# Scaling w_in on VectorE, and transposing the attention output by DMA from the third block of 512 tokens on

## The chip, the cores and the metric

One core of a Trainium2 chip. The metric is the device time of one launch in microseconds (us). All runs told of here were correct against the reference and fell in the fast state (a run over 1.5% above the fastest of the same kernel would be called slow). The profile covers one execution; its span is about 1.7 us shorter than the time of that launch. The two profiled launches compared first, 353.62 us before and 342.93 after, are each some 1.1 us faster than the median of their kernel. Shorthand in profile lines: PE is TensorE's matmuls, PEld its weight loads, DVE VectorE, ACT ScalarE, POOL GpSimd, SP the engine that issues the transfers (SPq its queue); L117 is line 117 of that kernel's source.

## The reference

```python
scores = q @ k.T / sqrt(64)                  # 8 batches, 8 heads, 576 positions, 64 per head
attn   = softmax(scores masked to 0 <= row - column < 64)
x      = (attn @ v), heads side by side      # 4608 tokens x 512
out    = (relu(x @ w_in) ** 2) @ w_out       # w_in 512 x 2048, w_out 2048 x 512
```

## The kernel before

The 4608 tokens are handled in 36 attention blocks of 128 tokens, `i`, four of which make one of the nine feed-forward blocks of 512 tokens, `g`. Four things matter.

The weights: `w_in` comes as sixteen tiles of 128x512 through four staging buffers, and each is scaled and cast.

```python
ws = wst.tile([P, FQ], FP32, name="ws", tag="ws")          # wst: bufs=4
nc.sync.dma_start(out=ws[:], in_=moe_w_in[c * P:(c + 1) * P, quar * FQ:(quar + 1) * FQ])
nc.gpsimd.tensor_scalar(out=w_in_sb[:, c, quar * FQ:(quar + 1) * FQ], in0=ws[:],
                        scalar1=W_SCALE, scalar2=None, op0=ALU.mult)
```

The attention of one block of 128 tokens: `transposes` (q and k), `scores` (with ScalarE's exponential and VectorE's mask, `pm`), `values` (giving `x_sb`), and last the transposition of `x_sb`, which the up-projection needs as `xT`:

```python
def to_xT(i):
    xt = ps_att.tile([P, DMC, P], FP16, name="xt_ps", tag="ps_a")
    for c in range(DMC):                                   # DMC = 4
        nc.tensor.transpose(out=xt[:, c, :], in_=xs[i][:, 2 * c:2 * c + 2, :], identity=ident[:])
    nc.vector.tensor_copy(out=xT_of(i // 4)[:, :, (i % 4) * P:(i % 4 + 1) * P], in_=xt[:])
```

The feed-forward: `ffn_up(g)` makes 16 groups of four matmuls (`hps`), each followed by a relu on ScalarE (`hrelu`) and a product on VectorE (`h`), over two accumulators. `ffn_out(g)` makes four output tiles of sixteen matmuls (`ops`), also over two accumulators, each emptied by ScalarE (`osb`).

The order: the first eight attention blocks (`NFIRST`) run in a start phase, with a quarter-wide up-projection per block (`ffn_up_chunk`). Then comes one stage per feed-forward block, in which streams are woven together:

```python
load(0)
for s in load_w_in():
    s()
for i in range(1, NV - 1):
    load(i)
...
for s in load_w_out() + ffn_up_chunk(0):
    s()
T(1), S_(1), warm(2), V(1), T(2), warm(2), X(1), S_(2)     # attention of block 1
...
for g in range(1, NTB + 1):
    streams = [(ffn_out(g - 1), 0.0, 1.0)]
    if g >= 2 and g < NTB:
        streams.append((ffn_up(g), 0.0, 1.0))
    if g + 1 < NTB:
        streams.append((attention(g + 1), 0.0, 0.95))
    if g + 2 < NTB:
        streams.append((loads(g + 2), 0.0, 1.0))
    for s in weave(*streams):
        s()
```

This is the order in which the program is written. The builder then orders each engine's instructions by itself, so a change of one operation can move others; "built order" below means what came out of that.

The softmax here doesn't subtract the row's maximum and nothing guards it: scores larger than these inputs give would overflow.

## Time and profile before

| | before |
|---|---|
| time, median of 3 runs | 354.94 us (354.49 to 355.84) |
| span of the profiled run | 351.9 us |
| last of the sixteen w_in scalings starts | 32.0 us, on GpSimd |
| TensorE busy in the whole span | 329.0 us, idle 22.9 us |

What bounds it is told in the prediction, with its lines. For the comparison a cut into three stretches is more useful than fixed times. The cuts are the starts of ScalarE's eviction of the fourth output tile (end of the first stage) and of the twelfth (end of the third stage). Columns of this table of windows: from:to, length, then busy us with the instruction count for PE, PEld, DVE, ACT and POOL, then granted clock, DMA share, GB/s.

```profile
0.00:98.41 98.41, 79.46 (x1062) 57.26 (x1064) 51.11 (x144) 39.59 (x69) 79.03 (x115) 0.90 0.85 218
98.41:169.69 71.28, 71.16 (x678) 36.56 (x678) 49.55 (x123) 36.95 (x67) 29.45 (x47) 1.00 0.54 129
169.69:351.90 182.21, 178.36 (x1412) 87.18 (x1410) 99.87 (x225) 87.62 (x154) 36.35 (x60) 1.00 0.33 88
```

Length minus TensorE's busy time is its idle time: 18.95 us in the first stretch, 0.12 in the second, 3.85 in the third. The second stretch is as full as a stretch can be, and so it is the one to watch when work is taken out of it. How the output matmuls of stage 2 (operand `h_1087`) lie in it is seen in the group of those instructions, with duration min/median/max in ns and the first and last start:

```profile
L296 PE MATMUL ops<-w_out_sb,h_1087 x64: 379/379/390, 98.8 to 135.2; 128*128 128x512 f16 x64
```

They are spread over 36 us, between the up-projection's matmuls of the same stage. While one group of four up-projection matmuls waits for relu and product, TensorE has output matmuls to do.

### The profile page before, as it was taken

Reading aid. Unit: us, or ns where it says so; the run is one execution under the profiler, and the core shown is the slowest. Engines: PE = TensorE matmul, PEld = TensorE weight load, DVE = VectorE, ACT = ScalarE, POOL = GpSimd, SP = SyncE. Lnnn points to the kernel's source line nnn. Section 1 sums busy time; section 2 is a strip of 40 time slices with the busy share of each in tenths; the row PEclk is TensorE's granted clock in tenths of the full one; section 3 lists DMA queues with packets and bytes.
Section 4 is the critical chain, followed back from the end, with each engine's and each line's share of the span. In section 5 each row is a group of like instructions: output and inputs, shape, how many; then the busy total and the mean of one; then the engine's idle time right before and its main releaser. Section 6 shows DMA issues by size and latency. Waiting matters only on the chain.

```text
span 351.9 us, 7908 instructions
## 1 busy us (share of the span) xinstructions
PE 329.0 (93%) x3146; PEld 181.0 (51%) x3146; DVE 200.5 (57%) x490; ACT 164.2 (47%) x289; POOL 144.8 (41%) x220
## 2 busy tenths in 40 slices
PE   4837898999999999999999999999999999999995
PEld 1424687885554555544554454445445544444442
DVE  3222588883385586767576756665676566633300
ACT  2112357553536554654555355536653664344411
POOL 4999997569575123324476464550000000000000
PEclk9965699999999999999999999999999999999999
DMA  7658999799895435536697675920000000100021
GB/s 199 187 166 205 214 231 263 241 228 246 214 218 121 121 85 141 125 88 165 162 219 180 160 179 139 215 68 33 30 32 32 31 32 32 59 31 32 31 80 69
DMA packets 122340, 46.64 MB, mean 133 GB/s; under 512 B 113600, under 2 KB 113600, under 8 KB 122304
## 3 DMA queue, kind: packets, MB, share of 16 engines
q1 hardware_dynamic: 122304, 46.15, 51.2%
q8 instruction: 24, 0.39, 0.5%
q14 instruction: 12, 0.10, 0.1%
HBM read 36.70 MB, written 9.44 MB: 131 GB/s over the span
## 4 chain that ended last, share of the span: by engine, by line
PE 82%; POOL 7%; DVE 4%; ACT 3%; DMA 1%; issue 1%; SPq 1%; ACTq 0%; POOLq 0%
PE ops L296 36%; PE hps L250 28%; POOL w_in_sb L117 7%; PE qkT_ps L173 4%; PE av L211 4%; PE xt_ps L224 2%; DMA ws<-in_moe_w_in_dram 1%; DVE h_397 L276 1%; DVE h_1087 L276 1%; SPq L151 1%; PE hps_639 L271 1%; PE hps_506 L271 0%; DVE x_sb L216 0%; DVE xT L226 0%; DVE kT L180 0%
## 5 line engine op out<-in xcount | busy, mean ns | idle before, releaser
L250 PE MATMUL hps<-xT,w_in_sb 128*128 128x512 f16 x448 | 115.2, 379 | 0.0
L254 ACT ACTIVATE hrelu<-hps 128x512 f32<-128x512 f32 x112 | 66.8, 598 | 91.4 <-PE hps L250 90.6
L250 PEld LDWEIGHTS <-w_in_sb 128*128 128x128 f16 x448 | 43.8, 98 | 52.6 <-issue 0.3
L271 PEld LDWEIGHTS <-w_in_sb 128*128 128x128 f16 x512 | 33.4, 104 | 15.7 <-POOL w_in_sb L117 11.7
L301 ACT ACTIVATE osb<-ops 128x512 f32<-128x512 f32 x36 | 21.6, 599 | 29.1 <-PE ops L296 29.1
L182 ACT ACTIVATE qT<-qkT_ps 128x512 f16<-128x512 f16 x36 | 21.5, 597 | 19.5 <-DVE kT L180 19.4
L180 DVE COPY kT<-qkT_ps 128x512 f16<-128x512 f16 x36 | 15.2, 421 | 25.3 <-PE qkT_ps L173 25.3
L216 DVE TENSOR_TENSOR x_sb<-av,rden 128x256 f16<-128x256 f32 x72 | 27.5, 416 | 0.1
L117 POOL TENSOR_SCALAR w_in_sb<-ws 128x512 f16<-128x512 f32 x16 | 23.5, 1492 | 1.0 <-DMA ws<-in_moe_w_in_dram 0.9
L226 DVE COPY xT<-xt_ps 128x512 f16<-128x512 f16 x36 | 15.1, 420 | 13.2 <-PE xt_ps L224 13.2
L215 DVE RECIPROCAL rden<-av 128x4 f32<-128x4 f32 x72 | 11.3, 178 | 16.5 <-PE av L211 16.2
L255 DVE SCALAR_TENSOR_TENSOR h_5222<-hps,hrelu 128x512 f16<-128x512 f32 x16 | 11.1, 692 | 16.6 <-ACT hrelu L254 16.6
L191 PEld LDWEIGHTS <-kT 64*128 64x128 f16 x576 | 11.3, 96 | 12.9 <-issue 10.9
L296 PE MATMUL ops<-w_out_sb,h_1087 128*128 128x512 f16 x64 | 17.5, 380 | 0.0
L296 PE MATMUL ops<-w_out_sb,h_2041 128*128 128x512 f16 x64 | 16.5, 380 | 0.0
L296 PE MATMUL ops<-w_out_sb,h_4199 128*128 128x512 f16 x64 | 16.5, 380 | 0.0
L296 PE MATMUL ops<-w_out_sb,h_3658 128*128 128x512 f16 x64 | 16.5, 380 | 0.0
L296 PE MATMUL ops<-w_out_sb,h_3120 128*128 128x512 f16 x64 | 16.5, 380 | 0.0
L296 PE MATMUL ops<-w_out_sb,h_2579 128*128 128x512 f16 x64 | 16.5, 380 | 0.0
L296 PE MATMUL ops<-w_out_sb,h_4736 128*128 128x512 f16 x64 | 16.4, 379 | 0.0
L224 PE MATMUL xt_ps<-ident,x_sb 128*128 128x128 f16 x144 | 15.0, 221 | 0.3 <-DVE x_sb L216 0.3
L296 PE MATMUL ops<-w_out_sb,h_397 128*128 128x512 f16 x64 | 15.3, 380 | 0.0
(837 smaller groups left out, 620.1 us busy)
## 6 DMA issues: line engine op xcount, KB each, us to landing
out_dram<-osb SPq DMA_DIRECT2D x36, 256.0 KB, 2.2
k_st<-in_k_dram SPq DMA_DIRECT2D x32, 256.0 KB, 4.0
q_st<-in_q_dram SPq DMA_DIRECT2D x32, 256.0 KB, 4.0
v_st<-in_v_dram SPq DMA_DIRECT2D x32, 256.0 KB, 4.1
ws<-in_moe_w_in_dram SPq DMA_DIRECT2D x16, 256.0 KB, 3.6
k_st<-in_k_dram SPq DMA_DIRECT2D x8, 128.0 KB, 3.3
q_st<-in_q_dram SPq DMA_DIRECT2D x8, 128.0 KB, 3.1
v_st<-in_v_dram SPq DMA_DIRECT2D x8, 128.0 KB, 3.1
```

Source lines behind the costliest of these rows:

```text
L117: nc.gpsimd.tensor_scalar(out=w_in_sb[:, c, quar * FQ:(quar + 1) * FQ], in0=ws[:], scalar1=W_SCALE, scalar2=None, op0=ALU.mult)
L173: nc.tensor.transpose(out=ps[:, s, hp, :], in_=src[i][:, hp * P:(hp + 1) * P], identity=ident[:])
L180: nc.vector.tensor_copy(out=kT[:, :, 64:192], in_=ps[:, 0])
L182: nc.scalar.activation(out=qT[:], in_=ps[:, 1], func=AF.Copy, scale=1.0)
L216: nc.vector.tensor_tensor(out=x_sb[:, 4 * half:4 * half + 4, :], in0=av[:, :, 0:D], in1=rden[:].to_broadcast([P, 4, D]), op=ALU.mult)
L224: nc.tensor.transpose(out=xt[:, c, :], in_=xs[i][:, 2 * c:2 * c + 2, :], identity=ident[:])
L226: nc.vector.tensor_copy(out=xT_of(i // 4)[:, :, (i % 4) * P:(i % 4 + 1) * P], in_=xt[:])
L250: nc.tensor.matmul(hps[:], w_in_sb[:, c, f * P:(f + 1) * P], xT_of(g)[:, c, :], start=(c == 0), stop=(c == DMC - 1))
L254: nc.scalar.activation(out=hrelu[:], in_=hps[:], func=AF.Relu)
L271: nc.tensor.matmul(hps[:, f, :], w_in_sb[:, c, (4 * fq + f) * P:(4 * fq + f + 1) * P], xT_of(g)[:, c, t0:t0 + P], start=(c == 0), stop=(c ...
L296: nc.tensor.matmul(hold["ps"][:], h2s[g][:, f, ts * P:(ts + 1) * P], w_out_sb[:, f, :], start=(f == 0), stop=(f == FFC - 1))
L301: nc.scalar.activation(out=osb[:], in_=hold["ps"][:], func=AF.Copy, scale=OUT_SCALE)
```

## The change

Its intent: take a slow elementwise operation off the engine that sets the start, and take 28 of the 36 transpositions of `x_sb` off the engine that sets the rest, giving them to a DMA path that has time. The attention is woven into 0.85 of a stage instead of 0.95, to leave the transfers time to land. Its core:

```diff
-            nc.gpsimd.tensor_scalar(
+            nc.vector.tensor_scalar(
                 out=w_in_sb[:, c, quar * FQ:(quar + 1) * FQ], in0=ws[:],
...
+    def to_xT_dma(i):
+        nc.sync.dma_start_transpose(
+            out=xT_of(i // 4)[:, :, (i % 4) * P:(i % 4 + 1) * P],
+            in_=xs[i][:].rearrange("p h d -> p (h d)"))
...
-        fns = (transposes, scores, values, to_xT)
+        fns = (transposes, scores, values, to_xT_dma)
...
-            streams.append((attention(g + 1), 0.0, 0.95))
+            streams.append((attention(g + 1), 0.0, 0.85))
```

## The prediction

> **What bounds the kernel now.** I read the page of the profile in this order: the busy line, the 40 slices, the chain that ended last, and then, with the trace, that chain in order of time and a table of the engines by stage.
>
> ```profile
> span 351.9 us, 7908 instructions
> ...
> PE 329.0 (93%) x3146; PEld 181.0 (51%) x3146; DVE 200.5 (57%) x490; ACT 164.2 (47%) x289; POOL 144.8 (41%) x220
> ...
> PE   4837898999999999999999999999999999999995
> ...
> POOL 4999997569575123324476464550000000000000
> PEclk9965699999999999999999999999999999999999
> DMA  7658999799895435536697675920000000100021
> ...
> PE 82%; POOL 7%; DVE 4%; ACT 3%; DMA 1%; issue 1%; SPq 1%; ACTq 0%; POOLq 0%
> ```
>
> There are two regimes. From the eighth slice on (62 us) TensorE is at 9 up to the last, and it is 82% of the chain. Before that it has holes, with a low granted clock in the third to fifth slice (18 to 44 us) and GpSimd full at the same time: the 7% of GpSimd in the chain belong there. The chain up to 40 us, in order of time, shows what GpSimd does in it:
>
> ```profile
> 2.91 4.54 DMA ws<-in_moe_w_in_dram
> ...
> 7.53 1.49 POOL w_in_sb L117
> ...
> 10.44 4.40 POOL w_in_sb L117 x3
> ...
> 15.39 1.45 POOL w_in_sb L117
> ...
> 17.41 7.27 POOL w_in_sb L117 x5
> ...
> 24.74 8.81 POOL w_in_sb L117 x6
> ...
> 33.60 1.58 PE hps_506 L271 x13
> ```
>
> The sixteen scalings of w_in follow each other on GpSimd at 1.49 us each, from 7.5 to 33.5 us, with only four other casts and copies between them. The last one releases the last quarter of the first up-projection. So the first 33 us are set by GpSimd. The table by stage (PE, PEld, DVE, ACT, POOL busy with counts, clock, DMA share, GB/s):
>
> ```profile
> 10.00:20.00 10.00, 6.29 (x67) 3.25 (x61) 2.94 (x8) 1.68 (x3) 9.91 (x9) 1.00 0.57 165
> 20.00:34.00 14.00, 8.25 (x63) 5.16 (x64) 3.34 (x6) 2.99 (x5) 13.94 (x11) 0.54 0.68 191
> ...
> 45.00:60.00 15.00, 13.31 (x258) 11.91 (x257) 13.06 (x32) 9.35 (x17) 12.90 (x22) 1.00 1.00 249
> ...
> 133.00:166.00 33.00, 33.00 (x298) 16.43 (x296) 21.77 (x51) 17.72 (x32) 12.16 (x20) 1.00 0.49 121
> ```
>
> The reader should see that GpSimd has no gap up to 34 us while the DMA engines are only 57 to 68% busy (they reach 249 GB/s later), and that in a later stage TensorE has 33.00 of 33.00 us while VectorE has 11 us to spare and the DMA half its time. What the removed transposes cost, and how the SP queue waits now:
>
> ```profile
> 75.30 0.22 PE xt_ps L224 x4
> ...
> L226 DVE COPY xT<-xt_ps 128x512 f16<-128x512 f16 x36 | 15.1, 420 | 13.2 <-PE xt_ps L224 13.2
> ...
> SPq L303 <- ACT osb L301: 183.3, 34, 8.5
> SPq L115 <- POOL w_in_sb L117: 15.2, 12, 2.0
> ```
>
> The four transposes of a token block of 128 advance the chain by 0.22 us, 55 ns each. Their 219 ns in the group list is latency, not occupancy. SP, which issues every transfer, waits 183 us for output tiles, so it has room for more issues; and in the start it waits 15.2 us for GpSimd to free a w_in staging buffer.
>
> **What the Trainium skill says.** TensorE: Matmul & The Clock Gate, "Wait — 56ns, not 53.3ns?": back-to-back matmuls with 128 moving columns start 55.6 ns apart when warm; the trace's 55 ns agrees. VectorE: DVE Perf Modes, "Mode 2×_2P — use both read ports for one tensor": a tensor_scalar from fp32 in SBUF makes two results per cycle. No such instruction is in this trace; 512 columns would be 267 ns at its 0.96 GHz, and with a start cost as in the trace's short VectorE operations I estimate 0.35 us, against GpSimd's 1.49. The same page, "The three transpose paths": the DMA crossbar takes 1309 ns for a 128x128 bf16 block, TensorE 390. Advanced Engine Details and Errata, "X-Bar Transpose (TRN2)", calls transposing transfers as fast as regular ones. The two last do not quite fit together, and no transposing transfer is in this trace.
>
> **The change part by part.**
>
> Part 1, w_in on VectorE. GpSimd loses 16 x 1.49 = 23.8 us, VectorE gains 16 x 0.35 = 5.6 us, at a time when it is a third busy or less. What then sets the end of w_in? Four staging buffers: SP may issue tile n only when tile n-4 is scaled, and a tile lands a median 3.6 us after issue. Four in flight of 256 KB per about 4 us is 260 GB/s, near the best the trace shows. But VectorE runs in program order, and the built order interleaves the scalings with the first token block: tile 8 stands behind the first mask operation (which waits for ScalarE's exponential), tile 10 behind the first reciprocal, tile 12 behind the xT copy. That block gets later itself: the masks stand behind the first scaling on VectorE, so the warm-up matmuls that read one can start near 8.5 us and not at 6.1, and with twelve of them ahead of the first scores (eight before) the xT copy moves from 14.2 to about 19. Tile 16 reuses the buffer of tile 12, so it is issued at about 19.5, lands at 23 to 24.5 and is scaled by 25; before, the last scaling ended at 33.5. That is 8 to 8.5 us. SP then gets to the remaining q, k, v loads at about 20 us and not at 28.1, also 8 us earlier, so what follows (seven chunks of up-projection and attention, 88% or more TensorE) finds its data in the same relation to time as before. Part of the clock loss stays[...]. Sum of part 1: 8 us, from 5 to 10.
>
> Part 2, blocks 2 to 8 transposed by the DMA. 7 x 4 = 28 token blocks: TensorE loses 28 x 4 = 112 of 144 transposes, 28 x 0.22 = 6.2 us, all of it in stages where TensorE is full, hence all on the path. VectorE loses 28 copies of 0.42 us, 11.8 us, on no path. ScalarE: nothing. SP gets 28 transfers of 128 KB, 3.7 MB in all; at 200 GB/s that is 18 us of DMA time over 230 us, of which from 232 us on nine tenths are free.
>
> Part 3, attention woven into 0.85 of a stage and not 0.95. It moves TensorE work, it does not add any. It buys time for the transfer: in the built order, from the last value matmul of a block to the first up-projection matmul that reads its xT, there stand 44 matmuls of 512 columns and 8 transposes in a mid stage. At 0.2155 us (0.86 per four in the chain) and 55 ns this is 9.9 us; in the kernel before it was 6.9. For block 2 it is about 13 us, for the last block 9.5.
>
> Sum: 354.9 - 8.0 - 6.2 = 340.7; I say 341.
>
> **The rivals.**
>
> Rival A, the transposing transfer is too slow. The path is reciprocal and product (0.18 + 2 x 0.42 = 1.0 us), issue, transfer, then the matmuls. It has 9.9 us. A plain 256 KB load takes 4.0 us to land; if the transpose of 128 KB behaves like one, it is hidden with 4 to 5 us to spare. If its four 128x128 blocks go one after another at the skill's 1309 ns, it takes 5.2 us, and since the third and fourth of a block become ready 2 us apart, the fourth would land 1 + 2 x 5.2 - 2 = 9.4 us after its values: just hidden. At 7 us each, TensorE would wait some 3 us in each of seven stages and part 2 would be worth minus 15. For it: the page's own figure; against it: somebody chose 0.85 for this, and the other page's "as fast as regular". Time if true: 350 to 365, and far more if the issue itself holds SP for over 8 us, as four must fit in a stage of 33 us beside the loads.
>
> Rival B, the SP queue. It issues in order; a transpose waits for VectorE's x_sb, and loads stand behind it. A late load delays an attention block two stages on. Against it: fifteen staging buffers hold five token blocks, and SP already waits 183 us for output tiles without holding anything up. I expect no more than 1 us.
>
> Rival C, the start is bound by the DMA or by the in-order VectorE and not by GpSimd's 1.49 us. From 34 to 103 us the DMA share is 0.93 or more. If the DMA is the limit, the gain is what it left idle: over 24 us at about 0.64, some 8 us, so the same number from another side. If VectorE's order holds the scalings up more than I think (its waits for the first block are serial), part 1 falls to 3 to 4 us: time 345.
>
> **Range and chances.** Part 1 from 5 to 10 and part 2 from 5.5 to 6.5 give 338.5 to 344.5. A tenth or so for a slow start and another for small waits for the transpose push the upper end further than the lower: 335.5 to 350. Faster by over 2% means under 347.8, a gain of over 7.1 us: this holds if part 1 is right and part 2 is worth anything, or the other way round with a little of the first; it fails only if the transposes stall TensorE. 0.80. Within 2%: 0.11. Slower by over 2%: 0.09, rival A in its strong form.
>
> **What would show it.** For part 1: the last scaling near 25 us on VectorE at about 0.35 us each, GpSimd gone from the chain's first 34 us, the chunk phase shifted earlier by about 8 us with its length kept. For part 2: 32 transposes left, stages from 105 us on shorter by 0.9 us each (4 x 0.22), TensorE still at 9 in each slice, and no wait of an up-projection matmul on a transposing transfer. Wrong if: the transfer takes over 8 us to land, TensorE shows holes at the start of a stage, VectorE's scalings end after 30 us, or SP's issue of a transpose takes several us.

## The result, and the profile after

343.99 us median (342.93 to 345.42, 4 runs) against 354.72 us (354.30 to 355.84, 4 runs) of the kernel before on the same chip: ratio 0.9695, 95% interval 0.9650 to 0.9741, correct. Ratios here are the mean time of one kernel's fast runs over that of the other's of the same rounds, so not quite the ratio of the medians quoted. The changed kernel is 10.7 us faster; the prediction said 341.0, that is 13.9. A later repetition (after_again below) gave 0.9738.

The page of the changed kernel, the lines that answer to those of before:

```profile
span 341.2 us, 7757 instructions
...
PE   1967988999999999999999999999999999999995
...
POOL 4008896479420662723645472544000000000000
...
PE 80%; DVE 9%; DMA 5%; ACT 3%; issue 1%; SPq 1%; ACTq 0%
```

GpSimd is gone from the chain (7% before), and VectorE (9%, before 4%) and transfers (DMA 5%, before 1%) take its place, at the start above all. Four transfers of w_in, 18.5 us in sum, make up most of the chain's first 25 us: the four staging buffers let the next load start only when an earlier tile is scaled. TensorE's second and third slice (8.5 to 25.6 us) read 9 and 6, where before they read 8 and 3. The three stretches, cut at the same two evictions:

```profile
0.00:91.53 91.53, 75.46 (x1062) 54.81 (x1064) 58.15 (x160) 39.37 (x69) 54.85 (x95) 0.96 0.86 222
91.53:162.88 71.35, 69.65 (x630) 33.98 (x630) 44.59 (x111) 37.21 (x68) 28.46 (x45) 1.00 0.68 158
162.88:341.20 178.32, 174.78 (x1348) 83.90 (x1346) 93.11 (x209) 88.07 (x154) 39.31 (x64) 1.00 0.41 105
```

| stretch | length before | after | gain | TensorE busy | TensorE idle | matmuls removed |
|---|---|---|---|---|---|---|
| start to 4th tile | 98.41 | 91.53 | 6.88 | 79.46 to 75.46 | 18.95 to 16.07 | 0 |
| 4th to 12th tile (stages 2 and 3) | 71.28 | 71.35 | -0.07 | 71.16 to 69.65 | 0.12 to 1.70 | 48 |
| 12th tile to end | 182.21 | 178.32 | 3.89 | 178.36 to 174.78 | 3.85 to 3.54 | 64 |

The gains sum to 10.70 us, the difference of the two spans. They are those of one pair of executions, and the first of them is the least certain: of nine profiled builds with this start, the fourth tile came at 91.5 us here, the earliest, and at 94.0 in the latest; with the start of before it came at 98.4 here and at 100.9 in a2_dma_only below. Three things are to be read from the table.

First, the start. The same 1062 matmuls take 4.0 us less busy time, at a mean granted clock of 0.96 instead of 0.90, and TensorE idles 2.9 us less. The last scaling now starts at 25.4 us on VectorE:

```profile
L117 DVE TENSOR_SCALAR w_in_sb<-ws x16: 353/424/884, 7.0 to 25.4; 128x512 f16<-128x512 f32 x16
```

Second, the last stretch. 64 removed transposes are sixteen groups of four; at the 0.22 us that the prediction read in the chain, that is 3.5 us, and TensorE's busy time falls by 178.36 - 174.78 = 3.58, or 0.224 for each four. The four stages in it that still have attention are 33.13 us each instead of 34.03. The transfers that replace them are hidden: the group of transposing issues on SP's queue (ns), and the time from issue to landing (us):

```profile
L229 SPq DMA_TRANSPOSE xT<-x_sb x28: 1189/1216/2044, 88.5 to 289.5; - x28
...
DMA to landing us min/median/max: 2.3/2.4/4.5
```

Third, the middle stretch, where 48 transposes are gone and nothing is gained. The same group of output matmuls that took 36 us before:

```profile
L301 PE MATMUL ops<-w_out_sb,h_1087 x64: 376/379/390, 91.7 to 111.1; 128*128 128x512 f16 x64
```

Now the last of the 64 starts at 111.1 us. In the built order 128 output matmuls (stages 1 and 2) stand ahead of the first up-projection matmul of stage 2; before, 80 did. So the filler is spent before the work it should fill. The chain of the changed kernel there, in order of time (start, duration, what):

```profile
104.73 0.44 DVE kT L180
...
105.25 0.60 ACT qT L182
105.85 0.50 ACT osb L306
...
106.39 2.10 PE ops L301 x9
...
111.49 0.88 PE hps L255 x4
112.39 0.61 ACT hrelu L259
113.02 0.70 DVE h_2021 L260
...
113.77 1.04 PE hps L255 x4
```

Two holes are visible. From 104.7 to 106.4 TensorE gives nothing to the chain: the fourth output tile needs one of the two accumulators, and ScalarE, in order, empties it only after a copy of q that waits for the k copy on VectorE. And from 111.5 on, four up-projection matmuls, relu, product, four matmuls go round in 2.3 us with little beside them, because the two accumulators are both waiting and no output matmul is left. The groups themselves are not slower: in a stream a matmul of 512 columns starts 0.2155 us after the one ahead, while the trace shows each for about 0.38 us, so four that are followed by a pause show as 3 x 0.2155 + 0.38 = 1.03 us and four in a full stage as 0.86. That is how the 2.7 us (12 x 0.224) went: into waits. 1.58 us of them show as more idle time. The other 1.18 (busy time fell by 1.51 us and not by 2.69) hide in the busy time, which counts the shown end of the last matmul before each pause. Counted from start to start, the pauses of this stretch sum to 2.7 us more than before.

### The profile page after: what moved, and what is told of

It reads as the page before. It is cut to its first block, busy times and chain, and to the rows that moved or that the text cites. A ratio compares the mean times of both kernels' runs of the same rounds, so it can differ in the third digit from the quotient of the medians.

```text
span 341.2 us, 7757 instructions
## 1 busy us (share of the span) xinstructions
PE 319.9 (94%) x3034; PEld 172.7 (51%) x3034; DVE 195.8 (57%) x478; ACT 164.7 (48%) x289; POOL 122.6 (36%) x204
## 4 chain that ended last, share of the span: by engine, by line
PE 80%; DVE 9%; DMA 5%; ACT 3%; issue 1%; SPq 1%; ACTq 0%
PE ops L301 37%; PE hps L255 27%; DMA ws<-in_moe_w_in_dram 5%; PE av L211 4%; PE qkT_ps L173 4%; DVE h_1087 L281 1%; DVE h_397 L281 1%; DVE h_2021 L260 1%; DVE w_in_sb L117 1%; ACT hrelu L259 1%; DVE xT L226 1%; DVE kT L177 1%; PE hps_639 L276 1%; SPq L151 1%; DVE kT L180 0%
## 5 line engine op out<-in xcount | busy, mean ns | idle before, releaser
L255 PEld LDWEIGHTS <-w_in_sb 128*128 128x128 f16 x448 | 43.3, 98 | 52.1 <-issue 1.9
L276 PEld LDWEIGHTS <-w_in_sb 128*128 128x128 f16 x512 | 31.1, 99 | 7.7 <-issue 3.0
L306 ACT ACTIVATE osb<-ops 128x512 f32<-128x512 f32 x36 | 21.5, 596 | 26.5 <-PE ops L301 26.5
L182 ACT ACTIVATE qT<-qkT_ps 128x512 f16<-128x512 f16 x36 | 21.5, 596 | 25.4 <-DVE kT L180 25.2
L260 DVE SCALAR_TENSOR_TENSOR h_5082<-hps,hrelu 128x512 f16<-128x512 f32 x16 | 11.1, 691 | 16.6 <-ACT hrelu L259 16.6
L301 PE MATMUL ops<-w_out_sb,h_2021 128*128 128x512 f16 x64 | 17.0, 381 | 0.0
L260 DVE SCALAR_TENSOR_TENSOR h_4616<-hps,hrelu 128x512 f16<-128x512 f32 x16 | 11.0, 689 | 9.8 <-ACT hrelu L259 9.4
L301 PE MATMUL ops<-w_out_sb,h_3060 128*128 128x512 f16 x64 | 16.5, 380 | 0.0
L301 PE MATMUL ops<-w_out_sb,h_3578 128*128 128x512 f16 x64 | 16.5, 380 | 0.0
L301 PE MATMUL ops<-w_out_sb,h_4099 128*128 128x512 f16 x64 | 16.5, 380 | 0.0
L301 PE MATMUL ops<-w_out_sb,h_2539 128*128 128x512 f16 x64 | 16.5, 380 | 0.0
L301 PE MATMUL ops<-w_out_sb,h_4616 128*128 128x512 f16 x64 | 16.4, 379 | 0.0
L301 PE MATMUL ops<-w_out_sb,h_1087 128*128 128x512 f16 x64 | 15.5, 380 | 0.8 <-ACT osb L306 0.8
L260 DVE SCALAR_TENSOR_TENSOR h_4099<-hps,hrelu 128x512 f16<-128x512 f32 x16 | 11.0, 689 | 8.7 <-ACT hrelu L259 8.4
L260 DVE SCALAR_TENSOR_TENSOR h_3578<-hps,hrelu 128x512 f16<-128x512 f32 x16 | 11.0, 689 | 8.7 <-ACT hrelu L259 8.4
L260 DVE SCALAR_TENSOR_TENSOR h_3060<-hps,hrelu 128x512 f16<-128x512 f32 x16 | 11.0, 688 | 8.2 <-ACT hrelu L259 8.0
```

The source lines that it names most:

```text
L182: nc.scalar.activation(out=qT[:], in_=ps[:, 1], func=AF.Copy, scale=1.0)
L255: nc.tensor.matmul(hps[:], w_in_sb[:, c, f * P:(f + 1) * P], xT_of(g)[:, c, :], start=(c == 0), stop=(c == DMC - 1))
L260: nc.vector.scalar_tensor_tensor(out=h2s[g][:, f, :], in0=hps[:], scalar=0.0, in1=hrelu[:], op0=ALU.max, op1=ALU.mult)
L276: nc.tensor.matmul(hps[:, f, :], w_in_sb[:, c, (4 * fq + f) * P:(4 * fq + f + 1) * P], xT_of(g)[:, c, t0:t0 + P], start=(c == 0), stop=(c ...
L301: nc.tensor.matmul(hold["ps"][:], h2s[g][:, f, ts * P:(ts + 1) * P], w_out_sb[:, f, :], start=(f == 0), stop=(f == FFC - 1))
L306: nc.scalar.activation(out=osb[:], in_=hold["ps"][:], func=AF.Copy, scale=OUT_SCALE)
```

## The experiments

All twelve were correct. Each was timed beside the kernel before on the same chip; times in us.

| run | what | median | ratio to before, 95% interval |
|---|---|---|---|
| a1_scale_only | before, w_in on VectorE | 348.48 | 0.9825 (0.9796 to 0.9855) |
| a2_dma_only | changed, w_in on GpSimd | 351.65 | 0.9924 (0.9897 to 0.9951) |
| a3_weave85_pe | w_in on VectorE, 0.85, all transposes on TensorE | 348.96 | 0.9850 (0.9826 to 0.9873) |
| a4_dma_w95 | changed, 0.95 | 345.96 | 0.9747 (0.9720 to 0.9774) |
| b2_double | changed, each transposing transfer twice | 345.43 | 0.9738 (0.9718 to 0.9759) |
| b6_xsb6 | changed, six x_sb buffers | 344.51 | 0.9725 (0.9701 to 0.9749) |
| b8_both5 | six buffers, output matmuls of stage 2 held back | 343.93 | 0.9710 (0.9692 to 0.9728) |
| d1_s1_early | changed, scores of block 1 earlier | 343.41 | 0.9706 (0.9676 to 0.9735) |
| after_again | changed kernel, repeated | 345.39 | 0.9738 (0.9703 to 0.9772) |
| e3_lo30 | six buffers, TensorE in written order in stage 2 | 343.15 | 0.9673 (0.9641 to 0.9704) |
| d2_load1_first | changed, block 1 loaded before w_in | 341.28 | 0.9621 (0.9592 to 0.9650) |
| f1_combo | d2_load1_first and e3_lo30 together | 340.42 | 0.9604 (0.9591 to 0.9617) |

The kernel before ran at 354.3 to 354.9 in every call. The four a runs shared one chip and its runs of before, so did b2 to d1, and so did the next three; f1_combo ran on another. Only after_again, e3 and d2 have the changed kernel beside them. Its two ratios, 0.9695 and 0.9738 with overlapping intervals, are what the others are held against.

**The parts apart.** Theory: two independent parts, the scaling worth most. Rival: the parts share one loss or one gain, or the 0.85 does something by itself.

a1_scale_only, against the kernel before:

```diff
-            nc.gpsimd.tensor_scalar(
+            nc.vector.tensor_scalar(
```

> Part 1 alone: w_in scaled on VectorE, all transposes on TensorE, attention over 0.95 of a stage as before. Theory (the two parts add; part 1 is worth what the chain gained by 82 us, 81.7 - 74.8 = 6.9 us): 347.9, span near 345, TensorE's up-projection of chunk 1 starting near 31.7 us and not at 38.4. Rival (part 1 was worth the predicted 8 us or more and part 2 gave back some of it): 346.5 or less.

Measured 348.48. Its middle stretch is 71.17 us long with TensorE idle for 0.04 us of it, and its stages after that take 34.03 us as before. So the scaling alone acts in the start and nowhere else.

a2_dma_only, against the changed kernel:

```diff
-            nc.vector.tensor_scalar(
+            nc.gpsimd.tensor_scalar(
```

> Parts 2 and 3 alone: transposes of blocks 2 to 8 by the DMA, attention over 0.85, w_in on GpSimd as before. Theory: 10.7 - 6.9 = 3.8 us, so 351.1, not the predicted 6.2 us (348.7), with the same hole of TensorE early in stage 2 as in the changed kernel. Rival (the hole comes only when the start is earlier and the loads are pressed together): 348.7 and no hole.

Measured 351.65, 2.7 us under the kernel before. Its middle stretch is 72.22 us (before: 71.28), its last one 178.36 (before: 182.21). The transposes alone thus gain 3.9 us late and give back 0.9 in the middle. (This profiled launch, 353.2 us, is the slowest of its six, with a first stretch 2.5 us longer than before.) The two parts sum to 5.9 + 2.7 = 8.6 us (from the medians, before at 354.33), the changed kernel's two measurements against before are 10.7 and 9.5. The parts add, within what the runs tell apart.

a3_weave85_pe, against the changed kernel:

```diff
-        fns = (transposes, scores, values, to_xT_dma)
+        fns = (transposes, scores, values, to_xT)
```

> VectorE scaling and attention over 0.85 of a stage, but all transposes left on TensorE: part 3 without part 2. Theory (0.85 moves work and costs nothing; the hole of stage 2 belongs to the order that the builder makes for transfers): the same as part 1 alone, 347.9 within 0.7. Rival (pressing attention into 0.85 is what overloads ScalarE and VectorE in stage 2): 349.5 or more, a hole in every stage or in stage 2.

Measured 348.96 against 348.48 of a1, intervals overlapping. Weaving at 0.85 costs and gains nothing that the times tell apart; in the profile its middle stretch is 0.8 us longer than a1's (71.99).

a4_dma_w95, against the changed kernel:

```diff
-            streams.append((attention(g + 1), 0.0, 0.85))
+            streams.append((attention(g + 1), 0.0, 0.95))
```

> The changed kernel with attention over 0.95 of a stage again. The transposing transfer was seen to land 2.4 us after issue and there are 6.5 us of TensorE work between the last values and the first up-projection in stages 4 to 8. Theory: those stages are as short as with 0.85 (33.1 us); the built order for stages 2 and 3 is worse (all output matmuls ahead of the up-projection in both), so 1 to 2.5 us slower than the changed kernel, 345 to 346.5. Rival (0.85 was needed to hide the transfer): each of stages 4 to 8 grows by over 1 us, 349 or more.

Measured 345.96. Four of its stages from the 12th tile on take 33.43, 33.13, 33.13 and 33.13 us, so the later stages do not need the 0.85 to hide the transfer. Its middle stretch is 1.1 us longer (72.44), with 128 output matmuls ahead of the first up-projection matmul here too.

**Is the transfer the cost?** b2_double, against the changed kernel (the second transfer goes to a tile that nobody reads):

```diff
+    twice = const.tile([P, DMC, P], FP16, name="twice")
+    def to_xT_two(i):
+        to_xT_dma(i)
+        nc.sync.dma_start_transpose(out=twice[:], in_=xs[i][:].rearrange("p h d -> p (h d)"))
...
-        fns = (transposes, scores, values, to_xT_dma)
+        fns = (transposes, scores, values, to_xT_two)
```

> The changed kernel with every transposing transfer issued twice, the second into a tile that nobody reads: the suspected cost of the transfers doubled (28 more transfers, 3.7 MB, 1.2 us of SP each). Theory (the transfers and SP are off the path; only the built order of stages 2 and 3 costs): stages from 164 us on as long as in the changed kernel, 33.1 us; whole time within 1.5 us of it, and any loss in stages 2 and 3, where this build also puts all output matmuls ahead of the up-projection in stage 3. Rival (transfers or SP cost the missing 2.4 us of part 2): 2 us or more slower, spread over all stages.

Measured 345.43. With 56 transfers instead of 28, three of the four late stages are still 33.13 us (the first is 33.34), and a landing takes 2.4 us in the median for the first of a pair and 2.5 for the second. The ratio, 0.9738, is that of after_again. So neither the transfer nor SP's issue of it is what costs the missing time, and there is room for as much again.

**What empties TensorE in stage 2?** Theory: the built order, which spends the output matmuls early. Rival: SP stands in front of a transposing transfer, waiting for `x_sb`. In the changed kernel SP waits 11.4 us in two waits for VectorE's `x_sb` there, and behind it a k load comes so late that GpSimd waits 13.1 us for it.

b6_xsb6, against the changed kernel:

```diff
+    xsp = ctx.enter_context(tc.tile_pool(name="xsp", bufs=6))
...
-        x_sb = attw.tile([P, H, D], FP16, name="x_sb", tag="x_sb")
+        x_sb = xsp.tile([P, H, D], FP16, name="x_sb", tag="x_sb")
```

> The changed kernel with six buffers for the attention output, not three. TensorE's order is the same as in the changed kernel; only VectorE's order in stage 1 changes (the last attention output of block 2 no longer stands behind the masks of block 3), so SP is not held from 96 to 106 us and the loads behind it come earlier. Theory (the loss of stage 2 is TensorE's order: up-projection without output matmuls between, paced by ScalarE and VectorE): hole of stage 2 stays, gain under 0.8 us. Rival (SP's stop and the late loads make the hole): 1.5 us or more faster, 342.5 or less.

Measured 344.51. The wait of SP shrinks from 11.4 to 3.1 us, and the loss stays: TensorE is busy for 27.89 of 30 us from 103 to 133 us, and the middle stretch is 71.52 us. The rival falls: SP's wait is a companion, not the cause.

b8_both5: b6_xsb6, and step n of stage 2's output matmuls may only be queued after the up-projection's group n - 5.

```diff
+        def step(ts, fq):
+            n = 4 * ts + fq - 5
+            if g == 1 and n >= 0:
+                with tc.issue_after(ups[2][n].ins):
+                    one(ts, fq)
+            else:
+                one(ts, fq)
```

> Six buffers for the attention output, and in stage 2 the output matmuls are held to alternate with the up-projection as in the later stages (output step n is queued behind up-projection step n-5). Nothing else changes: same work, same transfers. Theory (the order of stage 2 cost 1.9 us): 1.3 to 2.0 us faster than the changed kernel, near 342.3, the wait for the last transposing transfer of block 2 taking at most 0.5 back. Rival (stage 2 is slow for another reason): same time within 0.5.

Now 84 output matmuls stand ahead of the first up-projection matmul. The same two windows of this run:

```profile
82.00:103.00 21.00, 18.90 (x259) 10.96 (x258) 11.52 (x36) 10.54 (x20) 8.95 (x15) 1.00 0.69 157
103.00:133.00 30.00, 29.91 (x228) 14.12 (x227) 18.39 (x43) 15.40 (x28) 13.64 (x22) 0.94 0.71 174
```

TensorE has no hole from 103 to 133 us, so the order does make that hole. But a hole of 2.1 us opens before it, where the scores wait 2.1 us for ScalarE's copy of q. Output matmuls that filled that wait now come later. And busy is not the same as fast: the 0.94 in the second line is the granted clock, which was 0.50 from 103.58 to 107.00 us, right after that hole, and 1.00 from then on (26.00 of 26.00 us busy). In these 3.42 us the matmuls of 512 columns start 0.43 us apart instead of 0.2155; by the clock's record that is an estimated 1.7 us lost.

The time, 343.93, is not told apart from b6 or from the changed kernel: the expected gain of 1.3 to 2.0 us did not come, and by time alone the rival's outcome did. The half clock is not all of it: the other three launches had a higher mean clock (0.984 and 0.985 against 0.980) and were only 0.4 to 0.6 us faster.

**Why is the start worth 6.9 and not 8?** The chain of the changed kernel from the last scaling to the second chunk, then that of the kernel before from the same point on:

```profile
25.52 0.34 DVE w_in_sb L117
...
25.91 0.91 PE hps_506 L276 x13
...
28.50 0.76 DVE pm_561 L201
...
30.47 0.74 PE xt_ps L224 x4
...
31.71 1.88 PE hps_639 L276 x16
```

```profile
37.13 0.74 PE xt_ps L224 x4
...
38.37 0.69 PE hps_639 L271 x5
```

The last matmuls of the first chunk (`hps_506`) end at 26.8 us instead of 35.2, 8.4 us earlier. The second chunk (`hps_639`) starts at 31.7 instead of 38.4, 6.7 earlier. Before, there were 3.2 us between the two; now there are 4.9. The reading: the attention of block 1 used to run while TensorE waited for w_in; now w_in is no longer late and that attention stands on the path. In TensorE's waits it shows as the longest one there:

```profile
PE av L211 <- DVE pm_558 L201: 1.4, 1, 1.4
```

d1_s1_early, against the changed kernel:

```diff
-    for s in load_w_out() + ffn_up_chunk(0):
+    up = ffn_up_chunk(0)
+    for s in load_w_out() + up[:3]:
         s()
-    T(1), S_(1), warm(2), V(1), T(2), warm(2), X(1), S_(2)
+    T(1), S_(1), up[3](), warm(2), V(1), T(2), warm(2), X(1), S_(2)
```

> The changed kernel with the scores of the second token block put ahead of the last quarter of the first up-projection, in the time in which TensorE waits for the last w_in tiles anyway. In the changed kernel the values of that block wait 1.8 us for VectorE's masks after the up-projection. Theory (this wait is what cut part 1 from 8.4 us at the end of the first chunk to 6.9): 1.0 to 1.8 us faster than the changed kernel. Rival (the loss comes from the cold clock or from the loads of q and v, which come when they come): under 0.5 us.

Measured 343.41, not told apart from b6 and b8 beside it or from the changed kernel: the expected 1.0 to 1.8 us did not show. The second copy into xT starts at 30.98 us in its profile against 31.23. The data are late: GpSimd waits 8.6 us for block 1's q, which is loaded behind most of w_in.

after_again is the changed kernel once more, as a control for the next two, on their chip:

> The changed kernel once more, as the control of the next two on the same chip: 343.5 to 345, and from the fourth to the twelfth output tile 71.3 us.

345.39, its three stretches 92.83, 71.44 and 178.33 us.

d2_load1_first, against the changed kernel: loads first, and scores before the first chunk.

```diff
     load(0)
+    load(1)
     for s in load_w_in():
         s()
-    for i in range(1, NV - 1):
+    for i in range(2, NV - 1):
         load(i)
...
+    T(1), S_(1)
     for s in load_w_out() + ffn_up_chunk(0):
         s()
-    T(1), S_(1), warm(2), V(1), T(2), warm(2), X(1), S_(2)
+    warm(2), V(1), T(2), warm(2), X(1), S_(2)
```

> The changed kernel with the q, k, v loads of the second token block issued ahead of w_in and its transposes and scores placed ahead of the first up-projection. Same bytes. The last scaling moves from 25.4 to 26.5 to 27.5 us, as 0.5 MB go ahead of it; but the attention of the second block is again hidden in the wait for w_in, as it was before the change. Theory (1.7 us of part 1 were lost because that attention came out of hiding): the fourth output tile at 91.0 us or earlier, 0.3 to 1.2 us under the control. Rival (the start is bound by the bytes, and whatever goes first pushes w_in back by as much): same or slower than the control.

341.28, ratio 0.9621 against 0.9738 for the control, intervals apart: 4.1 us, several times what was expected. It beats both kernels. Its second copy into xT starts at 27.36 us (control: 32.58), although the last scaling now starts at 30.2 (26.5 to 27.5 was expected). But most of this lead is soon lost: the second chunk starts 4.3 us ahead of the control's, the third 2.3, the fourth 1.3. In between, the chain runs through the next v, which is still loaded behind w_in and lands at 31.1 us. At the fourth output tile 1.2 us are left (91.66 against 92.83; 91.0 or earlier was expected), no more than executions of the same start differ by: 91.53 in the first profile of the changed kernel. So the attention out of the shadow delays the second chunk, but that it is why the start is worth 6.9 us and not 8 is not shown. What is steadier comes in the middle stretch (71.35 and 71.44 in the two profiles of the changed kernel); first the control, then this run:

```profile
92.83:164.27 71.44, 69.66 (x630) 34.05 (x630) 44.80 (x111) 37.21 (x68) 28.24 (x45) 1.00 0.67 160
91.66:161.43 69.77, 69.03 (x621) 33.77 (x618) 43.28 (x105) 36.53 (x65) 28.96 (x45) 1.00 0.67 158
```

TensorE's idle time in it is 0.74 us instead of 1.78. The built order tells why: 128 output matmuls still stand ahead of the up-projection, but after the transposes of q and k that fall into the third tile there are 19 in a row instead of 13. The fourth tile thus starts 1.3 us later after them (6 x 0.2155), and by then ScalarE has emptied its accumulator. The wait of 104.7 to 106.4 us told above is gone from the chain. So of the 2.8 us between the two profiled runs, 1.2 lie in the first stretch and 1.7 are a side effect on the built order, which the expectation did not have. Where the rest of the 4.1 us between the means comes from, these two profiles do not show. (TensorE's 9 fewer matmuls here are mostly moved ahead, to the first stretch, which has 12 more.)

e3_lo30: b6_xsb6, TensorE held to the written order in stage 2 alone, and the up-projection entering at 0.3 of that stage instead of at its start, so that its xT is there in time.

```diff
-            streams.append((ffn_up(g), 0.0, 1.0))
+            streams.append((ffn_up(g), 0.3 if g == 2 else 0.0, 1.0))
...
-        for s in weave(*streams):
-            s()
+        with tc.manual_schedule(engines={mybir.EngineType.PE}) if g == 2 else nullcontext():
+            for s in weave(*streams):
+                s()
```

> The changed kernel with six buffers for the attention output, and in stage 2 TensorE held to the written order, in which the up-projection starts at 0.3 of the stage (so some 6 us after the last values of block 2, long enough for the transfer that takes 1 us of VectorE, 1.2 us of issue and 2.4 to 4 us to land) and then alternates with the output matmuls. The earlier try with another hold kept the alternation but made TensorE wait 2.1 us for the transfer. Theory (order of stage 2, nothing else, cost the missing 2.7 us): from the fourth to the twelfth output tile 69.0 to 69.8 us and not 71.3, whole time 1.3 to 2.3 us under the control. Rival (the transfers make stages 2 and 3 slow in some other way, loads or the SP queue): within 0.7 us of the control.

343.15, ratio 0.9673 against the control's 0.9738, with intervals that touch at their ends. Its profile has TensorE at 30.00 of 30.00 us from 103 to 133, and 18.73 of 21.00 before it, as in b8: the middle stretch is 71.31 us and hardly shorter, where 69.0 to 69.8 were expected. (The 2.1 us that the expectation puts down to the transfer in b8 were the wait for ScalarE's copy of q told above.) Here too the clock halved right after the hole:

```profile
98.50:101.91 3.41, 3.41 (x18) 1.76 (x16) 2.19 (x7) 0.71 (x2) 1.42 (x3) 0.50 0.64 90
```

Half of 3.41 us, 1.7, taken off gives an estimate of 69.6 us for the stretch at full clock, within what was expected. That profiled run, at 345.37, is the slowest of its six. It and the next slowest (344.61) have a mean clock of 0.980, the four faster ones (341.69 to 343.38) 0.984 or 0.985. That fits a half clock in the two slow ones alone, but only one trace is kept. Why the clock fell is not shown: it followed a hole of over 2 us in b8 and e3, and no drop followed the pause of 1.2 us in the changed kernel.

f1_combo, both edits together:

> The block 1 loads moved ahead of w_in, and the stage 2 edit (six x_sb buffers, TensorE held to the written order in stage 2, up-projection entering at 0.3 of it), together. Alone they measured 0.9621 and 0.9673 of the kernel before, against 0.9738 for the changed kernel on the same chip. If the start and the stage 2 hole are two separate losses, the two gains (4.1 and 2.3 us) add: ratio 0.9555, about 339.0 us, TensorE full (29.9 or more of 30.0 us) from 103 to 133 us and the fourth to twelfth output tile in about 69 us or less. If the earlier loads already mended the hole (there were only 0.7 us of it left in that run), nothing is added: ratio 0.960 to 0.964, about 341.3 us. If the written order only moves the hole to 82 to 103 us, as in its own profile, and the earlier loads do not fill it, it loses: over 342.5 us, TensorE at 19 of 21 us in that window.

340.42, ratio 0.9604. It is the fastest run of the study, beside 0.9621 of d2 alone with overlapping intervals. The windows of its profile:

```profile
82.00:103.00 21.00, 19.91 (x260) 10.98 (x259) 13.04 (x43) 11.08 (x21) 11.18 (x19) 1.00 0.83 186
103.00:133.00 30.00, 30.00 (x241) 14.46 (x240) 18.70 (x40) 15.84 (x29) 17.15 (x28) 1.00 0.88 213
```

Of the three outcomes expected, the time is that of "nothing is added", while the window from 103 to 133 us is that of "the gains add". The middle stretch says more: 68.04 us, 3.24 less than before the change. Its granted clock is 1.00 throughout. That is the 2.7 us of the removed transposes and some more, of which the twelve attention matmuls that moved ahead of the cut, as in d2, are a part. So in this profile the 2.7 us that the changed kernel gives back are had in full, by an order that keeps output matmuls between the up-projection's. TensorE still idles 1.1 us there, once for a mask (0.9 us). The additive sum of 339.0 was not reached, because d2 had already regained over half of the same loss (1.67 us of the middle stretch against the control).

## Why the prediction was right or wrong

The verdict held, with 343.99 in the range of 335.5 to 350. By its steps:

- **What bounds the kernel: right.** GpSimd's scaling set the first 33 us, and once off it GpSimd is in no part of the chain.
- **Part 1, the scaling itself: right.** The last one was expected to be done by 25 us and starts at 25.4; one takes 0.424 us in the median where 0.35 was estimated (0.157 us beyond the 0.267 that the prediction counted for its columns, where it allowed 0.08), and a tile landed 4.5 us after its issue in the median, not 3.6. The first chunk ends 8.4 us earlier, as the 8 to 8.5 said.
- **Part 1, what follows it: sized too high.** The step "what follows finds its data in the same relation to time as before" failed: the second chunk starts only 6.7 us earlier, because the attention of block 1 came out of w_in's shadow. At the end of the first stage 6.9 us are left of 8.0 in this pair of profiles, and other executions of this start were up to 2.5 us later. What sets that size stays open, since d2_load1_first brought the second chunk forward and lost most of it again at the next late load.
- **Part 2, size per transposition: right.** 0.224 us per four is what TensorE's busy time fell by in the last stretch, 64 transposes for 3.58 us.
- **Part 2, "all of it in stages where TensorE is full, hence all on the path": the main failure.** For 16 of the 28 blocks it held (3.9 us). For the 12 whose transposes fell into stages 2 and 3 it did not (-0.07 instead of 2.7): the change made the builder place the output matmuls of stage 2 ahead of its up-projection, and TensorE was no longer full there. The instruction order of the changed kernel was at hand when the prediction was made and shows the 128 instead of 80; it was read for the gap before the transfer, not for what lies between the up-projection's groups.
- **Part 3: right that it moves work only** (a3 beside a1). That it is needed to hide the transfer was not so in the last four stages (a4).
- **Rival A, the slow transfer: refuted.** It lands in 2.4 us in the median, against 9.9 us of cover. b2_double shows room for twice as many.
- **Rival B, SP's queue: half seen.** SP did get held up, for 11.4 us, and a load behind it was late. It cost nothing that b6_xsb6 can tell.
- **Rival C: not the case in its strong form.** VectorE's in-order scalings ended when expected. Its other half, the DMA as the next limit, is in part what came: w_in's transfers are now most of the chain up to 25 us.

In sum 8.0 + 6.2 was expected (14.2, told as 341 after rounding), and 6.9 + 3.8 came.

## What to carry to other kernels

Work taken off the bound engine is only gained if that engine still has something to do at every moment afterwards. So after such a change, look in the built order at what lies between dependent groups, not only at whether the new transfer lands in time. When a late input comes earlier, look for what used to run in its shadow, and bring that work's own data forward too, and then the next work's, or the lead is lost there. Read the granted clock beside the busy time: TensorE can be busy throughout at half the clock. And cut the trace at the same milestones before and after: the instruction counts show what was removed, and busy and idle time show where it went.

## What the Trainium skill lacked or had wrong

- "VectorE: DVE Perf Modes", section "The three transpose paths", gives 1309 ns for one 128x128 block over the DMA crossbar. Here one transfer of four such blocks (128x512, fp16) landed 2.3 us after issue at best and 2.4 us in the median, so the four do not follow each other at that time (5.2 us). "Advanced Engine Details and Errata", section "X-Bar Transpose (TRN2)", which calls such transfers as fast as regular ones, fits better: plain loads of 128 KB land in 3.1 to 3.4 us here, though they come from HBM.
- No page gives the time for which a transposing transfer of this kind, from SBUF to SBUF, 128 KB, on Trainium2, holds the queue of the engine that issues it ("DMA: Bandwidth & Descriptors" has counts for other transposing transfers). Here it is 1.22 us in the median and up to 2.04, where a plain load of a w_in tile holds it for 0.33.
